# Routed attention and an ELU layer on one core: attention of batches 2 to 4 regrouped into blocks of six units, PSUM in three shared pair tiles

## The chip, the core and the metric

One Trainium2 chip, one core of it. The time is device microseconds (us) of one execution of the whole kernel. The engines of the core run side by side, each takes its own instructions in order, and they wait for each other on semaphores: TensorE (PE in the profile; its weight loads have a row of their own, PEld), VectorE (DVE), ScalarE (ACT), GpSimd (POOL) and SyncE (SP), which issues the transfers. TensorE writes its results to PSUM, which holds eight banks of 512 float32 values in each of 128 partitions.

## The reference, cut to what matters

```python
batch, n_heads, seq, head_dim, n_clusters = 4, 8, 768, 64, 16
q_assign = argmax(q_n @ c_n)            # nearest of 16 centroids, per head
k_assign = argmax(k_n @ c_n)
mask = q_assign[:, :, :, None] == k_assign[:, :, None, :]
scores = where(mask, (q @ k.T) / sqrt(64), -1e9)
attn = softmax(scores)
x = (attn @ v) laid out as (3072, 512)  # heads side by side
h = x @ w_in                            # 512 -> 2048
g = where(h > 0, h, exp(min(h, 0)) - 1)
out = g @ w_out                         # 2048 -> 512, (3072, 512)
```

All inputs arrive as 64-bit floats and are computed as float32 (a float32 product is two matmul instructions here).

## The kernel before

Two heads make a *pair*: four pairs in a batch, sixteen in all. A batch of 768 tokens is cut into two *halves* of 384 query columns, and the keys into six tiles of 128. A *unit* is one pair, one half and one key tile; a batch has 48 units.

`score` (L305) computes a unit. The product of q and k contracts over 64 rows, one head in the upper and one in the lower half of the array (L311, four instructions); a second product in bf16 (L320, two instructions) subtracts 2^80 where the clusters differ. ScalarE takes the exponential of both heads in one instruction (L328) into a tile `p` of SBUF (six of them). `add` (L330) sums the `p` of a half, on GpSimd in batch 1 and on VectorE later. `values` (L340) multiplies `p` by v (L345, four instructions, contraction over 128, 64 output columns for each head) and accumulates six units in one bank. `divide` (L356) sums over the keys with a product by ones (L360), copies the sums on ScalarE, inverts them on VectorE (L366) and scales the half on GpSimd (L368, L369).

The layer, `mlp` (L372), takes one half of a batch in 28 steps. Sixteen `hidden` steps (L377) compute 128 of the 2048 columns each: eight instructions (L383), then exponential on ScalarE (L392), clamp on GpSimd (L393), and the last step on VectorE (L398), which is issued one step late (`lag`) and reads PSUM again. Twelve `outer` steps (L403) multiply by `w_out`, eight instructions each (L413); four of them make 128 rows of the output, copied by ScalarE (L422) and stored.

`turn` (L225) transposes 128-row tiles of q or k by a matmul with the identity, three at a time; ScalarE copies q, VectorE copies k. `similar` (L238), `assign` and `masks` find the clusters. `prepare(b)` plans them for a batch, which happens during the batch before. Weights arrive as 64-bit words and are converted by `weight_steps` (L209) in pieces that go back and forth between VectorE (L185 to L192, L197) and GpSimd (L186, L198); batch 1 carries nearly all of them.

The order is written out by hand (`manual_schedule`): every engine executes in the order in which the loop at L462 issues. Batch 1's attention runs alone; attention of batch b runs beside the layer of batch b-1; the layer of batch 4 runs alone at the end. One turn of the loop (a *slot*) is one score unit, the late steps that are due (`values` two slots after its score, `divide` three), the planned preparation, and one or two steps of the layer:

```python
            for step in later.pop(now, []):
                step()
            ...
            upto = (n + 1) * len(steps) // slots
            for step in steps[done:upto]:
                step()
```

PSUM before: two score tiles of two banks (`ps_s`), two single banks shared by `turn`, `similar`, `divide` and `hidden` (`bank()`), one bank for `values` (`ps_o`), one for `outer` (`ps_f`). A tile is taken in turn, and the instruction that first writes it waits for the last reader of what it held.

Of the kernel before, what the change touches and what calls it, by code (L numbers as in the profile page):

```python
# [9 lines left out]
F32 = mybir.dt.float32  # L10
# [8 lines left out]
P = 128  # L19
# [41 lines left out]
def main_path(ctx, tc, c, q, k, v, centroids, moe_w_in, moe_w_out, out):  # L61
# [27 lines left out]
    def bank():  # L89
        return ps_b.tile([P, 512], F32, name="bank", tag="b")  # L90
# [60 lines left out]
    cps = bank()  # L151
# [71 lines left out]
    T, sim, hot, qm = {}, {}, {}, {}  # L223

    def turn(i, j, half):  # L225
        name = "qk"[j]
        if half == 0:
            T[i, j] = turned.tile([P, S], F32, name=f"{name}T", tag="turned")
        ps = bank()
        for t in range(HT):  # L230
            nc.tensor.transpose(ps[:, ts(t, P)], raw[name, i][:, half * HT + t], ident)  # L231
        to = T[i, j][:, half * HS : (half + 1) * HS]
        if j == 0:
            nc.scalar.copy(to, ps[:, :HS])
        else:
            nc.vector.tensor_copy(to, ps[:, :HS])  # L236

    def similar(b, j, half):  # L238
        if half == 0:
            sim[b, j] = route.tile([P, S], F32, name="sim", tag="sim", bufs=1)  # L240
        ps = bank()
        for x in range(2):
            for e in range(2):
                for g in range(2):
                    pr = 2 * g + x
                    at = 64 * e + 32 * g
                    nc.tensor.matmul(  # L247
                        ps[at : at + 32, :HS],
                        lhsT=cTz[:, pr, e].rearrange("p x c -> p (x c)"),
                        rhs=T[b * NPR + pr, j][:, half * HS : (half + 1) * HS],  # L250
                        start=(x == 0),
                        stop=(x == 1),
                    )
        nc.vector.transpose(sim[b, j][:, half * HS : (half + 1) * HS], ps[:, :HS])
# [25 lines left out]
    def prepare(b):  # L280

        plan = {}
        for pr in range(NPR):
            i = b * NPR + pr
            at = 2 * NT * pr
            for j in range(2):
                for half in range(2):
                    plan.setdefault(at + j, []).append(
                        lambda i=i, j=j, half=half: turn(i, j, half)
                    )  # L290
            if i + 2 < len(pairs):
                plan[at + 1].append(lambda i=i: (load("q", i + 2), load("k", i + 2)))
        for j in range(2):
            for half in range(2):
                plan.setdefault(6 * NPR * 2 - 10 + 2 * j + half, []).append(
                    lambda j=j, half=half: similar(b, j, half)
                )
            plan[6 * NPR * 2 - 9 + 2 * j].append(lambda j=j: assign(b, j))
        plan.setdefault(6 * NPR * 2 - 4, []).append(lambda: masks(b * NPR))
        return plan  # L300


    pu, osum, den, o_ps, xT = {}, {}, {}, {}, {}

    def score(i, half, kt):  # L305
        b, pr = pairs[i]
        s = ps_s.tile([P, 2, 512], F32, name="scores", tag="s")
        cols = slice(half * HS, (half + 1) * HS)
        for e in range(2):
            rows = slice(64 * e, 64 * e + 64)  # L310
            nc.tensor.matmul(  # L311
                s[:, e, :HS],
                lhsT=T[i, 1][rows, ts(kt, P)],
                rhs=T[i, 0][rows, cols],
                start=True,
                stop=False,
            )
        for e in range(2):
            rows = slice(64 * e, 64 * e + 64)
            nc.tensor.matmul(  # L320
                s[:, e, :HS],
                lhsT=hot[b, 1][rows, ts(kt, P)],
                rhs=qm[i][rows, cols],
                start=False,
                stop=True,
            )
        p = pu[i, half, kt] = probs.tile([P, 2, HS], F32, name="p", tag="p")
        nc.scalar.activation(p, s[:, :, :HS], Act.Exp, scale=SCALE)  # L328
# [11 lines left out]
    def values(i, half, kt):  # L340
        if kt == 0:
            o_ps[i, half] = ps_o.tile([P, 512], F32, name="o", tag="o")
        o = o_ps[i, half]
        for e in range(2):
            nc.tensor.matmul(  # L345
                o[64 * e : 64 * e + 64, :HS],
                lhsT=raw["v", i][:, e, kt],
                rhs=pu[i, half, kt][:, e],
                start=(kt == 0),
                stop=(kt == NT - 1),  # L350
            )
        if kt == NT - 1:
            x = xT[i, half] = xtp.tile([P, HS], F32, name="xT", tag="xT")
            nc.scalar.copy(x, o[:, :HS])

    def divide(i, half):  # L356
        s = osum.pop((i, half))
        d = bank()
# [13 lines left out]
    def mlp(b, half, last):  # L372

        g = {}
        lag = []

        def hidden(f):  # L377
            if last and f % 2:
                h = ps_s.tile([P, 2, 512], F32, name="h2", tag="s")[:, 0, :HS]
            else:  # L380
                h = bank()[:, :HS]
            for ch in range(KC):
                nc.tensor.matmul(  # L383
                    h,
                    lhsT=w_in[:, ch, ts(f, P)],
                    rhs=xT[b * NPR + ch, half],
                    start=(ch == 0),
                    stop=(ch == KC - 1),
                )
            t = g[f] = gtp.tile([P, HS], F32, name="gT", tag="gT")  # L390

            nc.scalar.activation(t, h, Act.Exp)  # L392
            nc.gpsimd.tensor_scalar(t, t, 1.0, 0.0, op0=Alu.min, op1=Alu.max)  # L393
            for step in lag:
                step()
            lag.clear()
            lag.append(
                lambda: nc.vector.scalar_tensor_tensor(  # L398
                    t, t, -1.0, h, op0=Alu.add, op1=Alu.max
                )  # L400
            )

        def outer(t, part, o):  # L403
            for step in lag:
                step()
            lag.clear()
            if part == 0:
                if last and t % 2:
                    o[t] = ps_o.tile([P, DM], F32, name="o2", tag="o")
                else:  # L410
                    o[t] = ps_f.tile([P, DM], F32, name="f", tag="f")
            for f in range(4 * part, 4 * part + 4):
                nc.tensor.matmul(  # L413
                    o[t],
                    lhsT=g[f][:, ts(t, P)],
# [4 lines left out]
            if part == 3:  # L420
                o_sb = work.tile([P, DM], F32, name="o_sb", tag="o_sb")
                nc.scalar.copy(o_sb, o[t])  # L422
# [5 lines left out]
        o = {}  # L428
        for f in range(FC):
            yield lambda f=f: hidden(f)  # L430
        for t in range(HT):
            for part in range(4):
                yield lambda t=t, part=part: outer(t, part, o)
# [20 lines left out]
    LAG = 2  # L454
    slots = 2 * NPR * NT
    later = {}
    now = 0

    def at(n, step):
        later.setdefault(n, []).append(step)  # L460

    for b in range(B + 1):  # L462
        steps = []
        if b > 0:
            for half in range(2):
                steps.extend(mlp(b - 1, half, b == B))
        plan = prepare(b + 1) if b + 1 < B else {}
        done = 0
        for n in range(slots):
            if b < B:  # L470
                i, half, kt = b * NPR + n // (2 * NT), (n // NT) % 2, n % NT
                if n % (2 * NT) == LAG + 2 and i + 1 < len(pairs):
                    load("v", i + 1)
                if n % (2 * NT) == 2 * NT - 4 and pairs[i][1] + 1 < NPR:
                    masks(i + 1)
                score(i, half, kt)
                eng = nc.gpsimd if b == 0 else nc.vector
                at(now + 1, lambda i=i, half=half, kt=kt, eng=eng: add(i, half, kt, eng))
                at(now + LAG, lambda i=i, half=half, kt=kt: values(i, half, kt))
                if kt == NT - 1:  # L480
                    at(now + LAG + 1, lambda i=i, half=half: divide(i, half))
            for step in later.pop(now, []):
                step()
            if b == 0:
                weigh(2)
            for step in plan.get(n, []):
                step()
            upto = (n + 1) * len(steps) // slots
            for step in steps[done:upto]:
                step()  # L490
            done = upto
            now += 1
            if b == 1:
                weigh(2)
# [13 lines left out]
    ps = bank()  # L508
# [227 lines left out]
```

## Time and profile before

| | before |
|---|---|
| median of 3 runs | 1280.72 us (1280.26 to 1280.73) |
| the profiled execution, its own time | 1280.53 us |
| span of that execution, first to last instruction | 1278.8 us |
| PE busy | 1132.8 us, 89% of the span |
| DVE, ACT, POOL busy | 494.5, 281.8, 296.7 us |
| mean granted clock of TensorE | 0.956 |

Busy time is the time in which an instruction of the engine is in the record; matmuls overlap, so a busy PE is not one at its peak. The time outside the span (1280.53 less 1278.8) is 1.7 us. In the rows further down the columns of a timeline are: start in us, length in us, engine, line, operation, output and inputs, shape, how many instructions of one kind follow each other, and in brackets how long the engine stood idle before them and what ended that.

### The profile page before, as it was taken

The page shows a single profiled execution, that of the slowest core. Times are in us where ns is not written, and L with a number is a line of the kernel's source. Part 1 is how long each engine was busy: PE and PEld are TensorE (multiplying, and loading weights), DVE is VectorE, ACT ScalarE, POOL GpSimd, SP SyncE. Part 2 cuts the span into 40 slices and gives each one's busy share as a digit, 9 for nine tenths or more (in the row PEclk, how much of TensorE's full clock was granted, in tenths as well). Part 3 has the DMA queues.
Part 4 walks back from the last instruction along what each step waited for, and adds up shares of the span by engine and source line. Part 5 has one row for each costly group of instructions (what it writes and reads, how often), then busy time and mean ns, then how long its engine had stood idle before and what let it go on. Part 6 is the DMA issues. An engine that isn't in the chain of part 4 may idle for free.

```text
span 1278.8 us, 10641 instructions
## 1 busy us (share of the span) xinstructions
PE 1132.8 (89%) x4291; PEld 486.1 (38%) x4291; DVE 494.5 (39%) x596; ACT 281.8 (22%) x475; POOL 296.7 (23%) x303
## 2 busy tenths in 40 slices
PE   4644444799999999999999999999999999999998
PEld 2211111244433443344434443344434443454553
DVE  5888888833321335223321335223322332220110
ACT  2221212232212221223212321222212321110110
POOL 2476666552110220012110210012111210110110
PEclk9877777899999999999999999999999999999999
DMA  9423233010101010010100000000000000000000
GB/s 225 122 83 104 73 111 91 30 37 1 37 17 46 1 37 9 9 46 1 37 17 21 1 13 9 8 21 1 13 17 21 1 1 15 11 1 17 9 1 27
DMA packets 62793, 42.75 MB, mean 33 GB/s; under 512 B 51472, under 2 KB 55568, under 8 KB 62736
## 3 DMA queue, kind: packets, MB, share of 16 engines
q1 hardware_dynamic: 62736, 41.98, 11.5%
q8 instruction: 36, 0.59, 0.2%
q14 instruction: 21, 0.17, 0.0%
HBM read 35.68 MB, written 6.29 MB: 33 GB/s over the span
## 4 chain that ended last, share of the span: by engine, by line
PE 78%; POOL 8%; DVE 7%; issue 4%; ACT 2%; SPq 1%; DMA 0%; ACTq 0%; POOLq 0%
PE f L413 25%; PE bank L383 24%; PE scores L311 10%; PE o L345 8%; POOL psum L336 4%; PE h L383 3%; PE o L413 2%; PE scores L320 2%; DVE r L366 1%; PE bank L360 1%; PE bank L247 1%; DVE ex L187 1%; PE bank L231 1%; DVE kT L236 1%; POOL w_out L198 1%
## 5 line engine op out<-in xcount | busy, mean ns | idle before, releaser
L413 PE MATMUL f<-w_out,gT 128*128 128x512 f32 x704 | 320.4, 602 | 4.1 <-ACT o_sb L422 4.1
L383 PE MATMUL bank<-xT,w_in 128*128 128x384 f32 x896 | 314.2, 496 | 8.3 <-DVE kT L236 5.2
L328 ACT ACTIVATE p<-scores 128x768 f32<-128x768 f32 x192 | 155.8, 812 | 370.5 <-PE scores L320 363.1
L383 PEld LDWEIGHTS bank<-xT,w_in 128*128 128x128 f32 x896 | 163.1, 190 | 150.9 <-DVE gT L398 23.9
L413 PEld LDWEIGHTS f<-w_out,gT 128*128 128x128 f32 x704 | 128.3, 190 | 181.5 <-issue 171.9
L393 POOL TENSOR_SCALAR gT<-gT 128x384 f32<-128x384 f32 x128 | 64.8, 506 | 528.4 <-ACT gT L392 528.4
L311 PE MATMUL scores<-qT,kT 64*128 64x384 f32 x768 | 179.6, 545 | 0.0
L345 PE MATMUL o<-p,v_raw 128*64 128x384 f32 x768 | 170.0, 522 | 0.0
L366 DVE RECIPROCAL r<-r 128x384 f32<-128x384 f32 x32 | 81.7, 2552 | 216.5 <-ACT r L365 216.5
L398 DVE SCALAR_TENSOR_TENSOR gT<-gT,bank 128x384 f32<-128x384 f32 x112 | 61.7, 551 | 260.6 <-POOL gT L393 260.6
L336 DVE TENSOR_TENSOR psum<-psum,p 128x768 f32<-128x768 f32 x96 | 105.3, 1097 | 91.8 <-ACT p L328 91.4
L392 ACT ACTIVATE gT<-bank 128x384 f32<-128x384 f32 x112 | 55.0, 491 | 301.1 <-PE bank L383 301.1
L368 POOL TENSOR_TENSOR xT<-xT,r 128x384 f32<-128x384 f32 x32 | 46.3, 1448 | 316.0 <-DVE r L366 316.0
L360 PE MATMUL bank<-psum,ones 128*64 128x384 f32 x128 | 31.8, 579 | 91.1 <-DVE kT L236 48.9
L311 PEld LDWEIGHTS scores<-qT,kT 64*128 64x128 f32 x768 | 59.1, 188 | 121.4 <-issue 119.3
L345 PEld LDWEIGHTS o<-p,v_raw 128*64 128x64 f32 x768 | 42.2, 138 | 92.5 <-issue 92.5
L320 PE MATMUL scores<-qm,hot 64*128 64x384 bf16 x384 | 64.0, 326 | 8.2 <-DVE qm L278 8.2
L336 POOL TENSOR_TENSOR psum<-psum,p 128x768 f32<-128x768 f32 x32 | 58.8, 1837 | 1.0
L187 DVE TENSOR_SCALAR ex<-words 128x512 uint32<-128x512 uint32 x32 | 50.2, 1567 | 21.9 <-POOL w_out L198 11.5
L236 DVE COPY kT<-bank 128x384 f32<-128x384 f32 x32 | 17.1, 554 | 83.8 <-PE bank L231 83.8
L360 PEld LDWEIGHTS bank<-psum,ones 128*64 128x64 f32 x128 | 7.0, 147 | 106.8 <-issue 62.5
L369 POOL TENSOR_TENSOR r_sum<-r_sum,r 128x384 f32<-128x384 f32 x32 | 47.5, 1485 | 0.0
(78 smaller groups left out, 575.0 us busy)
## 6 DMA issues: line engine op xcount, KB each, us to landing
words<-in_moe_w_in_dram SPq DMA_DIRECT2D x16, 512.0 KB, 3.9
words<-in_moe_w_out_dram SPq DMA_DIRECT2D x16, 512.0 KB, 3.5
q_raw<-in_q_dram SPq DMA_DIRECT2D x32, 192.0 KB, 3.7
k_raw<-in_k_dram SPq DMA_DIRECT2D x32, 192.0 KB, 4.0
v_raw<-in_v_dram SPq DMA_DIRECT2D x16, 384.0 KB, 4.1
out_dram<-o_sb SPq DMA_DIRECT2D x24, 256.0 KB, 2.0
cen<-in_centroids_dram SPq DMA_DIRECT2D x1, 32.0 KB, 1.8
```

The source lines that it names most:

```text
L187: nc.vector.tensor_scalar(ex, high, 20, 0x7FF, op0=Alu.logical_shift_right, op1=Alu.bitwise_and)
L311: nc.tensor.matmul(s[:, e, :HS], lhsT=T[i, 1][rows, ts(kt, P)], rhs=T[i, 0][rows, cols], start=True, stop=False,)
L320: nc.tensor.matmul(s[:, e, :HS], lhsT=hot[b, 1][rows, ts(kt, P)], rhs=qm[i][rows, cols], start=False, stop=True,)
L328: nc.scalar.activation(p, s[:, :, :HS], Act.Exp, scale=SCALE)
L336: eng.tensor_tensor(to, pu[i, half, 0] if kt == 1 else to, pu[i, half, kt], op=Alu.add)
L345: nc.tensor.matmul(o[64 * e : 64 * e + 64, :HS], lhsT=raw["v", i][:, e, kt], rhs=pu[i, half, kt][:, e], start=(kt == 0), stop=(kt == NT - 1),)
L366: nc.vector.reciprocal(r, r)
L383: nc.tensor.matmul(h, lhsT=w_in[:, ch, ts(f, P)], rhs=xT[b * NPR + ch, half], start=(ch == 0), stop=(ch == KC - 1),)
L392: nc.scalar.activation(t, h, Act.Exp)
L393: nc.gpsimd.tensor_scalar(t, t, 1.0, 0.0, op0=Alu.min, op1=Alu.max)
L398: lambda: nc.vector.scalar_tensor_tensor(t, t, -1.0, h, op0=Alu.add, op1=Alu.max)
L413: nc.tensor.matmul(o[t], lhsT=g[f][:, ts(t, P)], rhs=w_out[:, f], start=(f == 0), stop=(f == FC - 1),)
```

## The change

Batch 1 (b = 0 in the code) keeps its slots of one unit. From the second batch on the loop goes in steps of six units, that is one half of one pair. In each step all six `values` of the half before are issued, and its `divide` straight behind them, then six scores in a row, then their adds, and then a *group* of the layer: four `hidden` pairs (eight tiles of 128 columns) or six `outer` steps. The preparation steps are spread between the steps of the group. In batch 1 `values` stays two units behind; `add` is issued in the slot of its own score instead of the next, and `divide` directly behind the sixth `values`, one slot earlier.

PSUM becomes three tiles of two banks, taken in turn by scores, `hidden`, `turn`, `similar` and `divide`, and two fixed banks: `o_bank` for `values` and for the first and third output tile of `outer`, `f_bank` for the second. `hidden` now computes two tiles of 128 columns into one pair tile, and its three later steps take 768 elements instead of 384; `turn` transposes six tiles and copies once.

```diff
-    gtp = ctx.enter_context(tc.tile_pool(name="gtp", bufs=FC))
-    ps_s = ctx.enter_context(tc.tile_pool(name="ps_s", bufs=2, space=PSUM))
-    ps_b = ctx.enter_context(tc.tile_pool(name="ps_b", bufs=2, space=PSUM))
-    ps_o = ctx.enter_context(tc.tile_pool(name="ps_o", bufs=1, space=PSUM))
-    ps_f = ctx.enter_context(tc.tile_pool(name="ps_f", bufs=1, space=PSUM))
+    gtp = ctx.enter_context(tc.tile_pool(name="gtp", bufs=FC // 2))
+    short = ctx.enter_context(tc.tile_pool(name="short", bufs=3, space=PSUM))
+    long = ctx.enter_context(tc.tile_pool(name="long", bufs=1, space=PSUM))
+    o_bank = long.tile([P, 512], F32, name="o_bank")
+    f_bank = long.tile([P, 512], F32, name="f_bank")
+    def banks():
+        return short.tile([P, 2, 512], F32, name="banks", tag="banks")
...
+    def turn(i, j):
+        T[i, j] = turned.tile([P, S], F32, name=f"{name_of[j]}T", tag="turned")
+        ps = banks()
+        for t in range(NT):
+            nc.tensor.transpose(ps[:, t // HT, ts(t % HT, P)], raw[name_of[j], i][:, t], ident)
...
-    def score(i, half, kt):
+    def score(i, half, kts):
+        for kt in kts:
+            s = banks()
...
             nc.scalar.copy(x, o_bank[:, :HS])
+            divide(i, half)
...
+        def hidden(n):
+            h = banks()
+            for e in range(2):
+                for ch in range(KC):
+                    nc.tensor.matmul(
+                        h[:, e, :HS],
+                        lhsT=w_in[:, ch, ts(2 * n + e, P)],
...
+            nc.scalar.activation(t, h[:, :, :HS], Act.Exp)
+            nc.gpsimd.tensor_scalar(t, t, 1.0, 0.0, op0=Alu.min, op1=Alu.max)
+            finish()
+            lag.append(
+                lambda: nc.vector.scalar_tensor_tensor(
+                    t, t, -1.0, h[:, :, :HS], op0=Alu.add, op1=Alu.max
...
+        def outer(t, part):
+            o = f_bank if t == 1 else o_bank
...
+        for n in range(0, FC // 2, FC // 4):
+            yield [lambda n=n: hidden(n) for n in range(n, n + FC // 4)] + [finish]
+        for parts in (
+            [(0, 0), (0, 1), (0, 2), (0, 3), (1, 0), (1, 1)],
+            [(2, 0), (2, 1), (2, 2), (2, 3), (1, 2), (1, 3)],
+        ):
+            yield [lambda t=t, part=part: outer(t, part) for t, part in parts]
...
+    def flush(left):
+        while len(pending) > left:
+            values(*pending.pop(0))
...
+        G = NT if b else 1
+        for n in range(0, units, G):
+            if b:
+                flush(0)
             if b < B:
...
+                score(i, half, kts)
+                pending.extend((i, half, x) for x in kts)
...
+                for x in kts:
+                    add(i, half, x, nc.vector if b else nc.gpsimd)
+            if b == 0:
+                flush(2)
+                weigh(2)
+            beside = [step for m in range(n, n + G) for step in plan.get(m, [])]
+            main = groups[n // G] if b else []
+            done = 0
+            for m, step in enumerate(main):
                 step()
+                upto = len(beside) * (m + 1) // len(main)
+                for other in beside[done:upto]:
+                    other()
+                done = upto
```

## Rows read from the trace of the kernel before

**Rows 1.** The page: busy time, share of the span, instructions.

```profile
PE 1132.8 (89%) x4291; PEld 486.1 (38%) x4291; DVE 494.5 (39%) x596; ACT 281.8 (22%) x475; POOL 296.7 (23%) x303
```

**Rows 2.** Busy time of each engine by stretch (start:end, length, engines, clock, DMA).

```profile
0.00:260.00 260.00, 137.75 (x735) 51.52 (x735) 209.71 (x264) 56.45 (x89) 147.97 (x122) 0.79 0.37 103
...
836.00:1105.00 269.00, 267.27 (x962) 112.14 (x964) 79.28 (x83) 66.36 (x111) 42.10 (x48) 1.00 0.03 11
```

**Rows 3.** Timeline of PE, a slot with `hidden`, batch 3.

```profile
602.56 2.85 PE L383 MATMUL bank<-xT,w_in 128*128 128x384 f32 x8
605.34 0.92 PE L311 MATMUL scores<-qT,kT 64*128 64x384 f32 x4
606.09 0.33 PE L320 MATMUL scores<-qm,hot 64*128 64x384 bf16 x2
606.34 0.87 PE L345 MATMUL o<-p,v_raw 128*64 128x384 f32 x4
607.14 5.43 PE L383 MATMUL bank<-xT,w_in 128*128 128x384 f32 x16
```

**Rows 4.** Timeline of PE, `divide` and `values` in a row, then `outer`.

```profile
663.81 0.87 PE L360 MATMUL bank<-psum,ones 128*64 128x384 f32 x4
...
665.25 3.70 PE L413 MATMUL f<-w_out,gT 128*128 128x512 f32 x8
```

**Rows 5.** Timeline of PE at the end, the layer alone.

```profile
1115.27 2.74 PE L383 MATMUL h<-xT,w_in 128*128 128x384 f32 x8
1117.85 2.74 PE L383 MATMUL bank<-xT,w_in 128*128 128x384 f32 x8
```

**Rows 6.** Timeline of PE and PEld in narrow windows, inside one score unit.

```profile
605.76 0.49 PE L311 MATMUL scores<-qT,kT 64*128 64x384 f32 x2
...
605.44 0.19 PEld L311 LDWEIGHTS scores<-qT,kT 64*128 64x128 f32 x2
605.76 0.10 PEld L320 LDWEIGHTS <-hot 64*128 64x128 bf16 x2
```

**Rows 7.** Who PE waited for, 258 us to the end: us, times, longest.

```profile
PE bank L231 <- DVE kT L236: 5.2, 8, 0.7
PE bank L383 <- DVE kT L236: 5.2, 8, 0.7
PE f L413 <- ACT o_sb L422: 4.1, 6, 0.7
PE bank L383 <- ACT qT L234: 2.0, 8, 0.3
```

**Rows 8.** Timeline of DVE, batch 1: the first reciprocals, one of each half.

```profile
75.71 2.55 DVE L366 RECIPROCAL r<-r 128x384 f32<-128x384 f32 x1
...
106.83 2.55 DVE L366 RECIPROCAL r<-r 128x384 f32<-128x384 f32 x1 [1.88 <-ACT r L365]
...
135.43 2.55 DVE L366 RECIPROCAL r<-r 128x384 f32<-128x384 f32 x1
```

**Rows 9.** Timeline of POOL and of PE where batch 1 ends.

```profile
255.85 1.08 POOL L368 TENSOR_TENSOR xT<-xT,r 128x384 f32<-128x384 f32 x1 [4.22 <-DVE r L366]
...
259.73 7.48 POOL L336 TENSOR_TENSOR psum<-psum,p 128x768 f32<-128x768 f32 x4
...
260.35 0.88 PE L231 MATMUL bank<-ident,q_raw 128*128 128x128 f32 x6
```

**Rows 10.** Stretches right behind two waits of PE (columns as in rows 2).

```profile
72.60:78.60 6.00, 5.97 (x18) 1.72 (x18) 5.90 (x9) 1.39 (x3) 2.37 (x3) 0.51 0.31 90
...
242.50:246.00 3.50, 3.48 (x20) 1.19 (x22) 3.43 (x6) 0.00 (x0) 0.00 (x0) 0.54 0.00 0
```

**Rows 11.** Groups by line, 258 to 1105 us: busy us, mean ns.

```profile
L328 ACT ACTIVATE p<-scores 128x768 f32<-128x768 f32 x145 | 117.7, 812 | 283.6 <-PE scores L320 279.9 <-POOL gT L393 1.7 <-POOL psum L336 1.0
...
L398 DVE SCALAR_TENSOR_TENSOR gT<-gT,bank 128x384 f32<-128x384 f32 x96 | 52.9, 551 | 178.1 <-POOL gT L393 178.1
L393 POOL TENSOR_SCALAR gT<-gT 128x384 f32<-128x384 f32 x96 | 48.6, 506 | 404.2 <-ACT gT L392 404.2
```

More of the change, by code (lines that the diff above doesn't have):

```diff
@@ L150, in main_path @@
         nc.vector.tensor_scalar(cen2[:, e], cen, par[:, e : e + 1], None, op0=Alu.mult)
-    cps = bank()
+    cps = banks()[:, 0]
     nc.tensor.transpose(cps[:, :P], cen2.rearrange("p e d -> p (e d)"), ident)
@@ L223, in main_path @@
     T, sim, hot, qm = {}, {}, {}, {}
[L225 to L232, printed above, removed]
+    name_of = "qk"
+    def turn(i, j):
[3 more added lines that the diff above has]
+            nc.tensor.transpose(ps[:, t // HT, ts(t % HT, P)], raw[name_of[j], i][:, t], ident)
+        to = T[i, j].rearrange("p (h s) -> p h s", h=2)
@@ L233, in turn @@
         if j == 0:
-            nc.scalar.copy(to, ps[:, :HS])
+            nc.scalar.copy(to, ps[:, :, :HS])
         else:
[L236 to L254, printed above, removed]
+            nc.vector.tensor_copy(to, ps[:, :, :HS])
@@ new lines, in similar @@
+    def similar(b, j):
+        sim[b, j] = route.tile([P, S], F32, name="sim", tag="sim", bufs=1)
+        ps = banks()
+        for half in range(2):
+            cols = slice(half * HS, (half + 1) * HS)
+            for x in range(2):
+                for e in range(2):
+                    for g in range(2):
+                        pr = 2 * g + x
+                        at = 64 * e + 32 * g
+                        nc.tensor.matmul(
+                            ps[at : at + 32, half, :HS],
+                            lhsT=cTz[:, pr, e].rearrange("p x c -> p (x c)"),
+                            rhs=T[b * NPR + pr, j][:, cols],
+                            start=(x == 0),
+                            stop=(x == 1),
+                        )
+            nc.vector.transpose(sim[b, j][:, cols], ps[:, half, :HS])
@@ L286, in prepare @@
             for j in range(2):
[L287 to L290, printed above, removed]
+                plan.setdefault(at + j, []).append(lambda i=i, j=j: turn(i, j))
             if i + 2 < len(pairs):
@@ L293, in prepare @@
         for j in range(2):
[L294 to L298, printed above, removed]
+            plan.setdefault(6 * NPR * 2 - 10 + 2 * j, []).append(lambda j=j: similar(b, j))
+            plan.setdefault(6 * NPR * 2 - 9 + 2 * j, []).append(lambda j=j: assign(b, j))
         plan.setdefault(6 * NPR * 2 - 4, []).append(lambda: masks(b * NPR))
@@ L300, in prepare @@
         return plan
-    pu, osum, den, o_ps, xT = {}, {}, {}, {}, {}
-    def score(i, half, kt):
+    pu, osum, xT = {}, {}, {}
+    def score(i, half, kts):
         b, pr = pairs[i]
-        s = ps_s.tile([P, 2, 512], F32, name="scores", tag="s")
         cols = slice(half * HS, (half + 1) * HS)
[L309 to L328, printed above, removed]
+        for kt in kts:
+            s = banks()
+            for e in range(2):
+                rows = slice(64 * e, 64 * e + 64)
+                nc.tensor.matmul(
+                    s[:, e, :HS],
+                    lhsT=T[i, 1][rows, ts(kt, P)],
+                    rhs=T[i, 0][rows, cols],
+                    start=True,
+                    stop=False,
+                )
+            for e in range(2):
+                rows = slice(64 * e, 64 * e + 64)
+                nc.tensor.matmul(
+                    s[:, e, :HS],
+                    lhsT=hot[b, 1][rows, ts(kt, P)],
+                    rhs=qm[i][rows, cols],
+                    start=False,
+                    stop=True,
+                )
+            p = pu[i, half, kt] = probs.tile([P, 2, HS], F32, name="p", tag="p")
+            nc.scalar.activation(p, s[:, :, :HS], Act.Exp, scale=SCALE)
@@ L340, in values @@
     def values(i, half, kt):
-        if kt == 0:
-            o_ps[i, half] = ps_o.tile([P, 512], F32, name="o", tag="o")
-        o = o_ps[i, half]
         for e in range(2):
             nc.tensor.matmul(
-                o[64 * e : 64 * e + 64, :HS],
+                o_bank[64 * e : 64 * e + 64, :HS],
                 lhsT=raw["v", i][:, e, kt],
@@ L353, in values @@
             x = xT[i, half] = xtp.tile([P, HS], F32, name="xT", tag="xT")
-            nc.scalar.copy(x, o[:, :HS])
+            nc.scalar.copy(x, o_bank[:, :HS])
+            divide(i, half)
     def divide(i, half):
         s = osum.pop((i, half))
-        d = bank()
+        d = banks()[:, 0]
         for e in range(2):
@@ L372, in mlp, with finish @@
     def mlp(b, half, last):
[L374 to L388, printed above, removed]
-                )
-            t = g[f] = gtp.tile([P, HS], F32, name="gT", tag="gT")
-            nc.scalar.activation(t, h, Act.Exp)
-            nc.gpsimd.tensor_scalar(t, t, 1.0, 0.0, op0=Alu.min, op1=Alu.max)
+        g, lag = {}, []
+        def hidden(n):
+            h = banks()
+            for e in range(2):
+                for ch in range(KC):
+                    nc.tensor.matmul(
+                        h[:, e, :HS],
+                        lhsT=w_in[:, ch, ts(2 * n + e, P)],
+                        rhs=xT[b * NPR + ch, half],
+                        start=(ch == 0),
+                        stop=(ch == KC - 1),
+                    )
+            t = g[n] = gtp.tile([P, 2, HS], F32, name="gT", tag="gT")
+            nc.scalar.activation(t, h[:, :, :HS], Act.Exp)
[4 more added lines that the diff above has]
+                    t, t, -1.0, h[:, :, :HS], op0=Alu.add, op1=Alu.max
+                )
+            )
+        def finish():
             for step in lag:
@@ L396, in hidden @@
             lag.clear()
[L397 to L411, printed above, removed]
+        def outer(t, part):
+            o = f_bank if t == 1 else o_bank
             for f in range(4 * part, 4 * part + 4):
                 nc.tensor.matmul(
-                    o[t],
-                    lhsT=g[f][:, ts(t, P)],
+                    o,
+                    lhsT=g[f // 2][:, f % 2, ts(t, P)],
                     rhs=w_out[:, f],
@@ L421, in outer @@
                 o_sb = work.tile([P, DM], F32, name="o_sb", tag="o_sb")
-                nc.scalar.copy(o_sb, o[t])
+                nc.scalar.copy(o_sb, o)
                 nc.sync.dma_start(
@@ L452, in main_path @@
         weigh(1)
[L454 to L460, printed above, removed]
+    units = 2 * NPR * NT
+    pending = []
+    def flush(left):
+        while len(pending) > left:
+            values(*pending.pop(0))
     for b in range(B + 1):
-        steps = []
+        groups = []
         if b > 0:
             for half in range(2):
-                steps.extend(mlp(b - 1, half, b == B))
+                groups.extend(mlp(b - 1, half, b == B))
@@ L467, in main_path @@
         plan = prepare(b + 1) if b + 1 < B else {}
-        done = 0
-        for n in range(slots):
+        G = NT if b else 1
+        assert b == 0 or len(groups) == units // G
+        for n in range(0, units, G):
+            if b:
+                flush(0)
             if b < B:
                 i, half, kt = b * NPR + n // (2 * NT), (n // NT) % 2, n % NT
-                if n % (2 * NT) == LAG + 2 and i + 1 < len(pairs):
+                kts = range(kt, kt + G)
+                within = range(n % (2 * NT), n % (2 * NT) + G)
+                if 3 in within and i + 1 < len(pairs):
@@ L473, in main_path @@
                     load("v", i + 1)
-                if n % (2 * NT) == 2 * NT - 4 and pairs[i][1] + 1 < NPR:
+                score(i, half, kts)
+                pending.extend((i, half, x) for x in kts)
+                if 2 * NT - 3 in within and pairs[i][1] + 1 < NPR:
                     masks(i + 1)
[L476 to L479, printed above, removed]
@@ L480, in main_path @@
-                if kt == NT - 1:
-                    at(now + LAG + 1, lambda i=i, half=half: divide(i, half))
-            for step in later.pop(now, []):
-                step()
[L484 to L492, printed above, removed]
+                for x in kts:
+                    add(i, half, x, nc.vector if b else nc.gpsimd)
@@ new lines, in main_path @@
+            if b == 0:
[5 more added lines that the diff above has]
+            for m, step in enumerate(main):
+                step()
+                upto = len(beside) * (m + 1) // len(main)
+                for other in beside[done:upto]:
+                    other()
+                done = upto
+            for other in beside[done:]:
+                other()
@@ L493, in main_path @@
             if b == 1:
-                weigh(2)
+                weigh(2 * G)
     weigh(1000)
@@ L507, in main_path @@
     nc.vector.tensor_reduce(ok[:, 3:4], ok[:, 0:3], axis=Axis.X, op=Alu.min)
-    ps = bank()
+    ps = banks()[:, 0]
     nc.tensor.matmul(ps[:1, :1], lhsT=ok[:, 3:4], rhs=ones[:, :1], start=True, stop=True)
```

8 lines of the change are left out of this document (removed).

## Prediction

> **What bounds the kernel now.** I read the page first: TensorE is busy 89% of the span, the next engine 39% [rows 1]. The split by stretch then shows two different kernels. Up to 260 us TensorE is busy about half the time at a mean clock of 0.79, while VectorE works 210 of 260 us on the weight conversion; from there on TensorE is hardly ever idle and its clock is at the full level, 2.4 GHz: 267.27 of 269.00 us in batch 4 [rows 2]. So from batch 2 on only two things can save time: the short waits that are left, and matmul time that is no streaming. A busy row can't tell these apart, so I went to the starts in the timeline.
>
> An eight-instruction `hidden` step that stands between attention steps takes 605.34 - 602.56 = 2.78 us from its start to the next [rows 3]. The same step among its own kind takes 1117.85 - 1115.27 = 2.58 [rows 5]. The 0.20 is paid for coming from, or going to, instructions of another shape of the array (128x128, 64x128 for scores, 128x64 for values). For values the same can be read: one unit between others takes 607.14 - 606.34 = 0.80 [rows 3], but `divide` and a unit of values behind it, both 128x64 and both of four instructions, take together 665.25 - 663.81 = 1.44 [rows 4], so that the second costs 0.64. A score unit takes 606.34 - 605.34 = 1.00 [rows 3]. Inside it the first pair of instructions takes 605.76 - 605.34 = 0.42 [rows 3, 6], the second 606.09 - 605.76 = 0.33 [rows 3, 6], the bf16 pair 0.25 [rows 3], where half of 0.33 would do (one pass instead of two). The float32 pair behind the first one, and the bf16 pair behind that, start without a gap. The extra 0.10 at the head and 0.09 at the tail thus look like the change of shape, and a unit that follows its own kind should take 1.00 - 0.19 = 0.81.
>
> **The change, part by part.** *Fewer changes of shape.* Each of 144 slots of batches 2 to 4 now holds values, scores and a layer step, three changes. In blocks of six, one slot's worth of changes remains for every six slots, so 120 of 144 save 0.20 + (0.80 - 0.64 = 0.16) + (1.00 - 0.81 = 0.19) = 0.55 us: 66.0 us. For `outer` steps I take the same 0.20, since they have the shape of `hidden`. The 0.16 and 0.20 are measured on neighbours of one kind; no row shows a score unit directly behind a score unit. Bounds for that term: 0 (the unit keeps 1.00; 22.8 us less) and 0.19. I take 0.19, because inside the unit the pair behind the first already streams.
>
> Here a rule is to be weighed. Loads of weights run beside the streaming in the rows: the load for the second float32 pair begins at 605.44, while the first pair, in the same two halves of the array, streams until 605.76, and the bf16 load begins at 605.76 with the second pair's start [rows 6]. The Trainium skill, "TensorE: Matmul & The Clock Gate", section "Part 3: Packing small matmuls — row/col tiling", says that a weight load overlaps matmuls in flight only when it goes to other rows of the array. By that rule the first load of every unit stays exposed inside a block, score and values units would keep 1.00 and 0.80, and only 120 x 0.20 = 24.0 would be saved. Here the trace contradicts it, and I follow the trace.
>
> *PSUM.* The waits of TensorE from 258 us on are 5.2 + 5.2 + 4.1 + 2.0 = 16.5 us [rows 7]. 12.4 of them belong to `turn`, whose halves and the next `hidden` step wait for a copy out of one of two banks; 4.1 to `outer`, where the next output tile waits for the copy of the last. Now a `turn` has six transposes in one of three tiles and a `hidden` pair before and after it, and the three output tiles alternate over two banks. I count all 16.5 as gone (bound below: 8).
>
> What could be late next is a tile of the three. A `hidden` pair holds its tile through ScalarE (at most 0.81, the time of 768 elements), GpSimd (about 2 x 0.51) and VectorE (about 2 x 0.55), 2.9 us [rows 11], while two further pairs of 2 x 2.58 = 5.16 us run before the tile is wanted again: hidden, with 7 us to spare. That spare also covers VectorE's reciprocal of 2.55 [rows 8] and most of the five adds. A score needs the tile of the third before it: three units of 0.81 make 2.43, an exponential 0.81 [rows 11] plus the unit's own streaming 0.81, so 0.8 us to spare. ScalarE's pace, 6 x 0.81, equals TensorE's; if each hand-over cost it 0.05 more, it would still not use up the spare in six units. Values need `p` of a block whose exponentials ended a whole group ago; `divide` needs sums that VectorE made during that group. These wait for nothing, and without that cover a block would lose the five adds on its path. The copies out of PSUM and the larger steps of `hidden` lie on engines with 60% of their time free. The loads keep their order on SyncE, and stores still follow ScalarE's copy: nothing there is wanted within tens of us.
>
> *Batch 1.* Its slots stay. Its pace comes from the weight pieces that go between VectorE and GpSimd: from reciprocal to reciprocal a half takes 106.83 - 75.71 = 31.1 us, the next 135.43 - 106.83 = 28.6 [rows 8]. The longer ones, three of seven, end with VectorE idle for 1.88 us, because `divide` wanted a bank that a copy of k still held. With `divide` ahead of the turn that goes: up to 3 x 2.5 = 7.5. But GpSimd's scaling (1.08 and about as much for the sum) now stands ahead of the last step of a weight piece. I take 4 saved (bounds: 5 lost, 7.5 saved).
>
> *The seam behind batch 1.* Today TensorE goes on with batch 2's first layer steps at 260.35, while GpSimd is still adding: those adds end at 259.73 + 7.48 = 267.2 [rows 9]. Now the last `divide` of batch 1 stands ahead of everything of batch 2, and it needs the last add. One add of 7.48 / 4 = 1.87 moves into the 4.22 us in which GpSimd waits for a reciprocal [rows 9], so the adds end near 265.3, and TensorE loses 265.3 - 260.35 = 5 us (bounds: 3 and 7). Behind waits the clock was at its lower level, 1.2 GHz: a granted clock of 0.51 over 6.0 us in one place, 0.54 over 3.5 us in another [rows 10]. Half of such a stretch is lost, 1.8 to 3.0; I take 2.
>
> **Sum.** 66.0 + 16.5 + 4 - 5 - 2 = 79.5 us. The profiled execution took 1280.5 us, practically the median (1280.72); 1280.5 - 79.5 = **1201.0 us**.
>
> **Rivals.** *Half of it:* score units don't get faster in a row, for their bf16 pair is shorter (0.16) than the load that must come next (0.19 [rows 6]). For it: no row shows two units in a row. Against: the second float32 load begins 0.10 behind the unit's start (605.44 less 605.34 [rows 3, 6]), so loads follow each other faster than one lasts. 1201.0 + 22.8 = 1224. Chance 14%. *Each unit still pays its first load* (the rule above as a mechanism): 66.0 shrinks to 24.0, so 1243. The 0.64 of the second 128x64 unit and the overlapping loads speak against it. 5%. *More saved:* batch 1 gains its full 7.5, the seam costs 3 and no clock: 1192 and below. 9%. *A wait at each block,* some 2.5 us where scores first want tiles that VectorE's last `hidden` step, behind its reciprocal, still holds: 24 blocks, 1261; today's order gives VectorE's work 7 us to spare. With smaller waits 1213 to 1261: 6%. *Slower:* the three tiles serialise the `hidden` pairs, each waiting for the chain of the pair before, 2.9 us in 64 pairs: 186 us, or 1387; it decides the sign from 79.5 / 64 = 1.24 us for each pair. Against it stand two free tiles; for it only that a tile now waits for three engines at double the length. 3%. That the change does nothing at all (each wait comes back elsewhere): the order is fixed by hand and TensorE's queue is the path, so 2%.
>
> **Numbers.** The forecast, 1201, has 61%, with a range of its own of 1192 to 1213. With the half case and part of the next it makes 1187 to 1236 for 8 in 10. Less than 0.2% (2.6 us) can't be told from no change. Faster 0.94, same 0.02, slower 0.04.
>
> **What would show it.** Six score units in a row starting 0.81 apart, values 0.64, `hidden` pairs at 5.16; no waits for `turn` or `outer`; one wait of `divide` for GpSimd near 260, with a low clock behind it. Score starts 1.00 apart would prove the half case; waits of PE on VectorE's L398 step at the head of groups the slow ones. The prediction is most wrong if the 0.10 ahead of a first pair is a load and not a change of shape.

## The result and the profile after

| | before | after |
|---|---|---|
| median | 1280.72 us (4 runs, 1280.26 to 1283.5) | 1209.22 us (4 runs, 1207.73 to 1209.34) |
| ratio | | 0.9435, 95% interval 0.9418 to 0.9451 |
| span of the profiled execution | 1278.8 us | 1207.4 us |
| mean granted clock | 0.956 | 0.950 |

The kernel is 71.5 us faster; 79.5 were forecast. In the page's first part the busy share of TensorE has not moved, though the span is 71 us shorter, which is why a busy share could not be the argument [rows 1]:

```profile
PE 1078.6 (89%) x4291; PEld 522.1 (43%) x4291; DVE 499.6 (41%) x516; ACT 268.4 (22%) x395; POOL 284.9 (24%) x239
```

The timeline of PE in a block of batch 2, after (the columns are those of [rows 3]):

```profile
303.60 0.82 PE L232 MATMUL banks<-ident,k_raw 128*128 128x128 f32 x6
304.35 4.09 PE L339 MATMUL o_bank<-p,v_raw 128*64 128x384 f32 x24
308.27 0.82 PE L355 MATMUL banks<-psum,ones 128*64 128x384 f32 x4
309.01 0.92 PE L308 MATMUL banks<-qT,kT 64*128 64x384 f32 x4
309.76 0.33 PE L317 MATMUL banks<-qm,hot 64*128 64x384 bf16 x2
309.92 0.81 PE L308 MATMUL banks<-qT,kT 64*128 64x384 f32 x4
...
310.73 0.81 PE L308 MATMUL banks<-qT,kT 64*128 64x384 f32 x4
...
314.06 2.20 PE L375 MATMUL banks<-xT,w_in 128*128 128x384 f32 x6
```

Read the starts. Six values units take 308.27 - 304.35 = 3.92 us, 0.65 each, where one alone took 0.80 [rows 3]. The six scores take 314.06 - 309.01 = 5.05, and from unit to unit 310.73 - 309.92 = 0.81, where one alone took 1.00 [rows 3]. From the first to the second unit it is 0.91: that one still has the 0.10 at its head. A whole block, from values to values, can be read in batch 4, which prepares nothing:

```profile
786.57 4.09 PE L339 MATMUL o_bank<-p,v_raw 128*64 128x384 f32 x24
...
1030.81 4.09 PE L339 MATMUL o_bank<-p,v_raw 128*64 128x384 f32 x24
```

Eight blocks in 1030.81 - 786.57 = 244.24 us, 30.53 each; the same batch took 269 us before [rows 2]. The waits of TensorE from 258 us on, after:

```profile
PE banks L355 <- POOL psum L333: 4.3, 1, 4.3
PE banks L249 <- DVE sim L256: 2.8, 4, 0.7
```

All of the 16.5 us [rows 7] are gone. The first line is the seam behind batch 1. The second is new, and its larger part lies ahead of 258 us, at the start and at the end of batch 1. The timeline of PE there, after:

```profile
38.04 2.79 PE L249 MATMUL banks<-kT,cTz 128*32 128x384 f32 x16 [5.95 <-DVE sim L256]
...
225.25 1.50 PE L249 MATMUL banks<-qT,cTz 128*32 128x384 f32 x16
240.02 2.79 PE L249 MATMUL banks<-qT,cTz 128*32 128x384 f32 x16 [13.28 <-DVE sim L256]
...
251.70 2.79 PE L249 MATMUL banks<-kT,cTz 128*32 128x384 f32 x16 [3.31 <-DVE sim L256]
...
268.37 2.16 PE L339 MATMUL o_bank<-p,v_raw 128*64 128x384 f32 x12
274.86 1.55 PE L355 MATMUL banks<-psum,ones 128*64 128x384 f32 x4 [4.33 <-POOL psum L333]
276.34 1.65 PE L308 MATMUL banks<-qT,kT 64*128 64x384 f32 x4
```

Between the two halves of `similar` TensorE stands still for 13.28 us, until VectorE has transposed the first half; VectorE comes to that only behind pieces of the weight conversion. Its timeline, after:

```profile
239.39 0.58 DVE L256 STREAM_TRANSPOSE sim<-banks 128x384 f32<-128x384 f32 x1
```

The scores behind it in TensorE's order are late, and so are GpSimd's adds. The adds of the last half end at 274.8 (below), where 265.3 less the 4 us of gain was forecast, and TensorE comes to batch 2's first scores at 276.34. The timeline of POOL, after:

```profile
267.36 7.45 POOL L333 TENSOR_TENSOR psum<-psum,p 128x768 f32<-128x768 f32 x4
```

So the two parts of the run went different ways. Before, 1278.8 - 260.35 = 1018.4 us lay behind the point where batch 2 begins [rows 9]; after, 1207.4 - 276.34 = 931.1: 87 us less, 80.5 forecast. Up to that point it takes 16.0 us more, 1 forecast.

### The profile page after: what moved, and what is told of

Same layout as the page of the kernel before. It is cut to its first block, busy times and chain, and to the rows that moved or that the text cites. A ratio compares the mean times of both kernels' runs of the same rounds, so it can differ in the third digit from the quotient of the medians.

```text
span 1207.4 us, 10470 instructions
## 1 busy us (share of the span) xinstructions
PE 1078.6 (89%) x4291; PEld 522.1 (43%) x4291; DVE 499.6 (41%) x516; ACT 268.4 (22%) x395; POOL 284.9 (24%) x239
## 4 chain that ended last, share of the span: by engine, by line
PE 79%; DVE 8%; POOL 7%; issue 3%; DMA 1%; SPq 1%; ACT 0%; POOLq 0%; ACTq 0%
PE banks L375 28%; PE o_bank L401 18%; PE f_bank L401 9%; PE banks L308 9%; PE o_bank L339 9%; POOL psum L333 3%; PE banks L317 2%; PE banks L249 2%; DVE ex L189 2%; POOL w_out L200 1%; PE banks L355 1%; DVE ex L193 1%; DVE r L361 1%; PE banks L232 1%; DVE ex L192 1%
## 5 line engine op out<-in xcount | busy, mean ns | idle before, releaser
L375 PE MATMUL banks<-xT,w_in 128*128 128x384 f32 x1024 | 334.6, 488 | 0.0
L375 PEld LDWEIGHTS banks<-xT,w_in 128*128 128x128 f32 x1024 | 193.5, 190 | 137.4 <-issue 5.9
L401 PE MATMUL o_bank<-w_out,gT 128*128 128x512 f32 x512 | 224.9, 595 | 0.0
L325 ACT ACTIVATE p<-banks 128x768 f32<-128x768 f32 x192 | 153.9, 810 | 148.5 <-PE banks L317 142.4
L308 PE MATMUL banks<-qT,kT 64*128 64x384 f32 x768 | 172.9, 530 | 6.4 <-DVE kT L237 6.4
L401 PEld LDWEIGHTS o_bank<-w_out,gT 128*128 128x128 f32 x512 | 95.9, 190 | 119.1 <-issue 118.6
L339 PE MATMUL o_bank<-p,v_raw 128*64 128x384 f32 x768 | 145.4, 512 | 0.0
L401 PE MATMUL f_bank<-w_out,gT 128*128 128x512 f32 x256 | 112.9, 593 | 0.0
L308 PEld LDWEIGHTS banks<-qT,kT 64*128 64x128 f32 x768 | 67.7, 196 | 81.9 <-issue 65.9
L317 PE MATMUL banks<-qm,hot 64*128 64x384 bf16 x384 | 65.8, 336 | 29.4 <-DVE qm L280 29.4
L333 POOL TENSOR_TENSOR psum<-psum,p 128x768 f32<-128x768 f32 x32 | 58.7, 1834 | 10.3 <-ACT p L325 9.5
L189 DVE TENSOR_SCALAR ex<-words 128x512 uint32<-128x512 uint32 x32 | 43.8, 1368 | 32.3 <-POOL w_out L200 17.6
```

The lines of the kernel that those rows point to most:

```text
L189: nc.vector.tensor_scalar(ex, high, 20, 0x7FF, op0=Alu.logical_shift_right, op1=Alu.bitwise_and)
L308: nc.tensor.matmul(s[:, e, :HS], lhsT=T[i, 1][rows, ts(kt, P)], rhs=T[i, 0][rows, cols], start=True, stop=False,)
L317: nc.tensor.matmul(s[:, e, :HS], lhsT=hot[b, 1][rows, ts(kt, P)], rhs=qm[i][rows, cols], start=False, stop=True,)
L333: eng.tensor_tensor(to, pu[i, half, 0] if kt == 1 else to, pu[i, half, kt], op=Alu.add)
L339: nc.tensor.matmul(o_bank[64 * e : 64 * e + 64, :HS], lhsT=raw["v", i][:, e, kt], rhs=pu[i, half, kt][:, e], start=(kt == 0), stop=(kt == ...
L375: nc.tensor.matmul(h[:, e, :HS], lhsT=w_in[:, ch, ts(2 * n + e, P)], rhs=xT[b * NPR + ch, half], start=(ch == 0), stop=(ch == KC - 1),)
```

## The experiments

The first four were timed beside each other, and the last three likewise; the kernel before took 1281.7 us in both sets. The changed kernel was timed only in the first comparison, where the kernel before took 1280.72, so the differences from its 1209.22 us below can be off by about 1 us.

**The two halves of `similar` issued ahead of the two transposes.**

```diff
                             stop=(x == 1),
                         )
-            nc.vector.transpose(sim[b, j][:, cols], ps[:, half, :HS])
+        for half in range(2):
+            cols = slice(half * HS, (half + 1) * HS)
+            nc.vector.transpose(sim[b, j][:, cols], ps[:, half, :HS])
```

> The changed kernel, but `similar` issues the matmuls of both halves before the two transposes on VectorE. Theory: the second half's matmuls waited for VectorE's transpose of the first half (13.3 and 3.3 us in batch 1, 6.6 us in the start, 0.7 us twice in each of two later batches) only because both halves now sit in one tile and the transpose stood between them; TensorE stood still and starved the adds of batch 1. Then these waits vanish, batch 1 ends 8 to 11 us earlier, and the time is about 1209.2 - 12 = 1197 (1194 to 1202). Rival: batch 1 is set by the pieces of the weight conversion between VectorE and GpSimd, and TensorE's wait is hidden; then 1206 to 1209.

Measured: 1196.51 us (1195.49 to 1197.13), ratio to before 0.9337 (0.9319 to 0.9355). 12.7 us come from the order of two transposes. Its timeline of PE:

```profile
222.77 2.79 PE L249 MATMUL banks<-qT,cTz 128*32 128x384 f32 x32
...
237.17 0.92 PE L310 MATMUL banks<-qT,kT 64*128 64x384 f32 x4 [3.40 <-DVE sim L258]
...
247.72 1.65 PE L310 MATMUL banks<-qT,kT 64*128 64x384 f32 x4 [6.88 <-DVE sim L258]
...
265.29 0.87 PE L357 MATMUL banks<-psum,ones 128*64 128x384 f32 x4 [4.23 <-POOL psum L335]
```

Both halves now run through in 2.8 us, the scores follow, and the `divide` of the seam is free at 265.29, 9.6 us earlier. About a third of this is there from the start: the first reciprocal of batch 1 begins at 75.73, in the changed kernel at 79.07 (shown with the old order below). The timeline of DVE in this experiment:

```profile
75.73 2.55 DVE L363 RECIPROCAL r<-r 128x384 f32<-128x384 f32 x1
```

The transpose reads one bank and the late matmuls write the other, so nothing in the data made them wait. It was the order: both halves are parts of one tile, and in this program a write to the tile that is issued behind a read of it waited for that read. Before, each half had a tile of its own. Not all waiting for these transposes is gone: 3.40 + 6.88 = 10.3 us are left in batch 1, now ahead of score units, whose PSUM tile comes free only behind a transpose.

**The last `divide` of batch 1 behind the first group of batch 2.**

```diff
+    late = []
...
-            divide(i, half)
+            if i == NPR - 1 and half == 1:
+                late.append(lambda: divide(i, half))
+            else:
+                divide(i, half)
...
             for other in beside[done:]:
                 other()
+            for step in late:
+                step()
+            late.clear()
```

> The changed kernel, but the `divide` of the last half of batch 1 is issued behind the first group of batch 2 instead of ahead of its first scores. Theory: the seam costs the 4.3 us in which TensorE waits for GpSimd's last add, and about 1.6 us at the lower clock behind it, so 1203 (1201.5 to 1205). Rival: the wait only moves, because the first `hidden` pair or the first scores then wait for something else at the seam: 1208 to 1210.

Measured: 1203.67 us (1203.04 to 1203.87), ratio 0.9390 (0.9373 to 0.9408): 5.5 us. Its timeline of PE at the seam shows values, scores and layer without a wait, and no slow instruction:

```profile
268.92 2.16 PE L340 MATMUL o_bank<-p,v_raw 128*64 128x384 f32 x12
271.00 0.92 PE L309 MATMUL banks<-qT,kT 64*128 64x384 f32 x4
...
276.05 10.59 PE L379 MATMUL banks<-xT,w_in 128*128 128x384 f32 x32
```

**Scores and values one by one inside the block.**

```diff
...
-                score(i, half, kts)
-                pending.extend((i, half, x) for x in kts)
+                old = len(pending) if b else 0
+                for x in kts:
+                    if old:
+                        values(*pending.pop(0))
+                        old -= 1
+                    score(i, half, [x])
+                    pending.append((i, half, x))
```

(The `flush(0)` at the head of the loop stays only for the layer alone at the end.)

> The changed kernel, but inside a block scores and values alternate one by one instead of six and six; groups of the layer, tiles and waits stay. Theory (the change of the array's shape costs what the rows said): five more changes to scores and five more to values in a block, 5 x (0.195 + 0.15) = 1.7 us in 24 blocks, 41 us: 1250 (1245 to 1256). Rival: the gain comes from the long runs of the layer and the tiles, not from runs of scores and values: 1209 to 1220.

Measured: 1249.57 us (1248.72 to 1250.89), ratio 0.9748 (0.9728 to 0.9768). 40.4 us are lost again with nothing changed but the order of these two. The units are back at the length they had before, 308.41 - 307.61 = 0.80 for values and 309.42 - 308.41 = 1.01 for scores; the timeline of PE in this kernel:

```profile
307.61 0.87 PE L339 MATMUL o_bank<-p,v_raw 128*64 128x384 f32 x4
308.41 0.92 PE L308 MATMUL banks<-qT,kT 64*128 64x384 f32 x4
...
309.42 0.87 PE L339 MATMUL o_bank<-p,v_raw 128*64 128x384 f32 x4
```

**The new tiles and wider steps, but slots of one unit throughout.**

```diff
...
-            o = f_bank if t == 1 else o_bank
+            o = o_bank if last and t == 1 else f_bank
...
-        G = NT if b else 1
+        G = 1
+        done = 0
...
+            flush(2 if b < B else max(0, 1 - n))
...
+            upto = (n + 1) * len(groups) // units
+            for step in groups[done:upto]:
+                step()
+            done = upto
```

(`hidden` is split into its two tiles of 128 columns again, eight instructions to a step, with one exponential behind the second.)

> The changed PSUM tiles, pair-wide `hidden` and whole `turn`, but slots of one unit in all batches as in the kernel before (`hidden` issued in two halves of eight instructions; `outer` on one bank, since `values` always has the other open). Theory: the blocks make the gain; without them only the waits of `turn`, 12.4 us, go, and batch 1 and the seam lose about 11, so 1279 (1268 to 1288). Rival: the tiles and the wider steps make a good part of the gain: 1245 or less.

Measured: 1273.58 us (1270.95 to 1274.84), ratio 0.9933 (0.9911 to 0.9956). The tiles without the blocks are worth 1281.7 - 1273.6 = 8.1 us, within the theory's range and far from the rival's. From here to the alternating blocks, that is from one layer step to a slot to runs of the layer, 1273.58 - 1249.57 = 24.0 us, and the sum had 120 x 0.20 = 24.0; from there to the changed kernel 40.4 us, and the sum had 120 x (0.16 + 0.19) = 42.0. These differences also hold what the kernels differ by at the seam. Batch 4 has neither a seam nor a preparation; its beginning and the beginning of what follows it in the timeline of PE, in this kernel:

```profile
830.59 0.92 PE L308 MATMUL banks<-qT,kT 64*128 64x384 f32 x4
...
1097.56 0.87 PE L339 MATMUL o_bank<-p,v_raw 128*64 128x384 f32 x4
```

and with the alternating blocks:

```profile
814.41 0.87 PE L339 MATMUL o_bank<-p,v_raw 128*64 128x384 f32 x4
...
1072.71 4.09 PE L339 MATMUL o_bank<-p,v_raw 128*64 128x384 f32 x24
```

It takes 266.97, then 258.30, and 244.24 us in the changed kernel: steps of 8.7 and 14.1, where a third of the sum's terms is 8.0 and 14.0.

**Batch 1's old order of adds and `divide`.**

```diff
...
-            divide(i, half)
+            if i < NPR:
+                due.append(lambda: divide(i, half))
+            else:
+                divide(i, half)
...
             if b == 0:
+                run(due)
                 flush(2)
+                run(adds)
+                adds.append(lambda i=i, half=half, kt=kt: add(i, half, kt, nc.gpsimd))
```

(`due` and `adds` are lists; `run` executes a list and empties it; what is left over is run ahead of batch 2's first block.)

> The changed kernel with batch 1's old order of adds and `divide` (each add one slot after its score, `divide` one slot later and ahead of the add). The prediction had taken 4 us of gain for batch 1; measured were halves of 29.9 us, against 31.1 and 28.6 in turn before, and no such gain. Theory: ahead of GpSimd's last step of a weight piece the scaling and the sum of `divide` now hold up the next piece; with the old order, and the bank of k's copy no longer in the way, every half takes 28.6, seven halves save 7 to 9 us: 1201 (1198 to 1204). Rival: the order doesn't matter, since a half is the length of four pieces of the conversion and a reciprocal in any order: 1206 to 1211.

Measured: 1202.17 us (1200.89 to 1203.31), ratio 0.9377 (0.9361 to 0.9392): 7.0 us. The rows of GpSimd and VectorE show where they are. The changed kernel, timeline of POOL:

```profile
111.67 1.31 POOL L363 TENSOR_TENSOR xT<-xT,r 128x384 f32<-128x384 f32 x1 [3.56 <-DVE r L361]
112.95 1.24 POOL L364 TENSOR_TENSOR r_sum<-r_sum,r 128x384 f32<-128x384 f32 x1
114.15 1.26 POOL L200 TENSOR_TENSOR w_in<-w_in,ex 128x512 f32<-128x512 f32 x1
```

This experiment, the same view:

```profile
136.01 1.27 POOL L200 TENSOR_TENSOR w_out<-w_out,ex 128x512 f32<-128x512 f32 x1 [2.15 <-DVE w_out L199]
138.47 1.05 POOL L373 TENSOR_TENSOR xT<-xT,r 128x384 f32<-128x384 f32 x1 [1.19 <-DVE r L371]
```

A weight piece ends with a step on VectorE (L199) and, behind it, one on GpSimd (L200), for which VectorE waits in the next piece. In the changed kernel `divide` stands inside a piece, on both engines: VectorE's step stands behind the reciprocal and begins at 111.51 (below); GpSimd's stands behind the scaling and the sum, ahead of which GpSimd idles 3.56 us, and begins at 114.15. In the old order both steps are done before: VectorE's begins at 135.25, ahead of the reciprocal, GpSimd's at 136.01. What each engine's share of the cost is the experiment doesn't show, since it moves both. The reciprocals of VectorE give the halves. The changed kernel, timeline of DVE:

```profile
79.07 2.55 DVE L361 RECIPROCAL r<-r 128x384 f32<-128x384 f32 x1
...
109.05 2.55 DVE L361 RECIPROCAL r<-r 128x384 f32<-128x384 f32 x1
111.51 0.63 DVE L199 SCALAR_TENSOR_TENSOR w_in<-words,w_in 128x512 f32<-128x512 uint32 x1
...
138.83 2.55 DVE L361 RECIPROCAL r<-r 128x384 f32<-128x384 f32 x1
...
228.53 2.55 DVE L361 RECIPROCAL r<-r 128x384 f32<-128x384 f32 x1
```

and this experiment:

```profile
78.31 2.55 DVE L371 RECIPROCAL r<-r 128x384 f32<-128x384 f32 x1
...
107.65 2.54 DVE L371 RECIPROCAL r<-r 128x384 f32<-128x384 f32 x1
...
135.25 0.68 DVE L199 SCALAR_TENSOR_TENSOR w_out<-words,w_out 128x512 f32<-128x512 uint32 x1
135.85 2.54 DVE L371 RECIPROCAL r<-r 128x384 f32<-128x384 f32 x1
```

30.0 and 29.8 us against 29.3 and 28.2, where the kernel before had 31.1 and 28.6 [rows 8]. The theory had said 28.6 for every half; the mean of these two, 28.8, is near it.

**Together.** First the orders of `similar` and of the seam:

> The changed kernel with `similar`'s matmuls ahead of its transposes and the seam's `divide` behind the first group. Theory: the two costs are separate and add up: 1209.2 - 12.7 - 5.5 = 1191 (1189 to 1193). Rival: with `similar` mended batch 1's end is set by GpSimd's adds anyway and the seam's wait was one with it: 1195 to 1197.

Measured: 1190.33 us (1189.47 to 1190.66), ratio 0.9287 (0.9272 to 0.9303). Then all three:

> All three together: `similar`, the late `divide` at the seam, and batch 1's old order of adds and `divide`. Theory: if the old order is worth 7 to 9 us by itself, about 1183 (1180 to 1187). Rival: 1190 to 1193, as without the old order.

Measured: 1183.91 us (1182.19 to 1184.29), ratio 0.9237 (0.9222 to 0.9253). The three alone gave 12.7, 5.5 and 7.0, together 25.2; the kernel with all of them is 25.3 us faster than the changed one. It is the fastest of this study.

## Why the prediction was right, and where it was off

- *Changes of shape, 66.0 us:* right in mechanism and size. The unmeasured 0.19 of a score unit was there: 0.81 from unit to unit, and the alternating order loses 40.4 us again. For these instructions this also settles the rule on weight loads: were the first load of each unit exposed, units in a row would have stayed at 1.00 and 0.80. The 0.10 at the head is paid only behind another shape, which is what the prediction named as its weakest point; whether it is an emptying of the array or a load that begins late because of the change, no run separates. The Trainium skill, "TensorEngine Tiling (Array Packing)", section "Key Properties", says that a change of the tiling mode, not of the tile, drains TensorE. The trace agrees in that time is lost only where the shape changes, and gives the price here: 0.15 to 0.20 us a change (0.20 around a layer step, 0.15 around a unit of values).
- *Waits, 16.5 us:* right; none of them is in the trace of after. New are 2.8 us in batches 2 and 3, for `similar`.
- Both together were too small by some 6 us. Batch 4 took 268.75 us before, from its first score at 835.89 to the first values behind it at 1104.64 in the timeline of PE, and takes 244.24 now: 24.5 saved, where a third of 66.0 and two of the six waits for `o_sb` make 23.4. In batches 2 and 3 a part is `turn`. The timeline of PE before, a turn of k and the step behind it:

```profile
266.05 0.55 PE L231 MATMUL bank<-ident,k_raw 128*128 128x128 f32 x3
267.25 0.55 PE L231 MATMUL bank<-ident,k_raw 128*128 128x128 f32 x3 [0.65 <-DVE kT L236]
268.45 2.85 PE L383 MATMUL bank<-xT,w_in 128*128 128x384 f32 x8 [0.65 <-DVE kT L236]
```

It took 268.45 - 266.05 = 2.40 us and takes 304.35 - 303.60 = 0.75: 1.65 less, where its two waits made 1.30. At 0.35 for each of eight turns of k this makes an estimated 2.8 us. Where the rest comes from stays open.
- *The seam, 5 + 2 us:* right in kind. The late `divide` gives 5.5 back: 4.3 of waiting, and some 1.2 from the clock, which was granted at 0.60 over the 4 us behind the wait; the prediction had bounded the clock's part at 1.8 to 3.0. That the wait is so near to 5 says little, since both GpSimd's last add and TensorE came to the seam some 10 us later than forecast.
- *Batch 1, 4 us saved:* wrong. The wait for the copy of k went, as said, but the price of a `divide` inside a weight piece, taken as 3.5 of 7.5, was nearly as large as the gain. From the first to the sixth reciprocal it took 226.25 - 75.71 = 150.5 us before and 228.53 - 79.07 = 149.5 after: five halves, with all three of the longer ones, and 1 us saved. The prediction had seen the price on GpSimd alone; the rows of the old order show it on VectorE too. The timeline of DVE before:

```profile
226.25 2.56 DVE L366 RECIPROCAL r<-r 128x384 f32<-128x384 f32 x1 [1.88 <-ACT r L365]
```

- *"What could be late next is a tile of the three":* the step that failed. The spare of each tile, from its last reader to its next writer, was worked out for batches 2 to 5, and no score and no `hidden` pair waits there. But only waits between users of a tile were looked for. `similar` writes a tile, reads it and writes its other half, and there the wait is inside one use. It costs 12.7 us, 9.6 of them up to the seam, some 3 at the start and some 6 at the end of batch 1. No term of the sum and no rival had it.
- The balance: 1201.0 + some 15 us up to the seam (9.6 for `similar`, 3 of the 4 of batch 1's gain, 2 to 3 not told apart) less 6.5 behind it makes 1209.5; measured 1209.2. That the time lies in the range of 1192 to 1213 is luck in part: the two misses have opposite signs, and without the 6.5 us behind the seam it would have been 1215.7.
- One sum of the prediction doesn't come out: *more saved* is 1201.0 - 3.5 - 2 - 2 = 1193.5, not 1192.

## What to carry to other kernels

Where TensorE is the path and its instructions alternate between shapes of the array, compare the start-to-start time of a step among its own kind with that of a step between others: here the difference was 0.15 to 0.20 us a change, and three changes in each of 144 slots were 79 us, 6% of the time. When small PSUM tiles are merged into larger ones, follow each tile through one use as well as from use to use: a write to one part that is issued behind a read of another part may wait for that read. Issuing all writes first took this wait away here, though the next user of the tile still waited for the reads. In a chain that goes back and forth between two engines, look where a foreign step falls: inside a link of the chain it can delay both engines, and between links it did so less here, by 7.0 us.

## What was not expected of the hardware

A short VectorE step slows down when GpSimd begins an add beside it. The same instruction twice in batch 1, and the add beside the second, after:

```profile
49.55 0.43 DVE L189 TENSOR_SCALAR ex<-words 128x512 uint32<-128x512 uint32 x1 [1.16 <-POOL w_in L200]
...
55.57 1.81 POOL L333 TENSOR_TENSOR psum<-psum,p 128x768 f32<-128x768 f32 x1
...
55.65 2.02 DVE L189 TENSOR_SCALAR ex<-words 128x512 uint32<-128x512 uint32 x1 [1.17 <-POOL w_in L200]
```

At 55.57 GpSimd begins an add of 1.81 us, and the 0.43 become 2.02: the VectorE step ends 0.3 us behind it. At 49.55 GpSimd runs only the one-operand step of a weight piece. Between 40 and 240 us of this trace L189 comes 27 times: 19 times it meets an add as it begins and takes 2.0 us, 8 times it doesn't and takes 0.4. The adds set the length there; what in the hardware holds the step up, no run shows. So in batch 1 the adds are not hidden beside the conversion, as their place on another engine suggests; no experiment here moved them away.
